# Routing attention with an MLP behind it: another start for the first batch

## Chip, cores, metric

One core of a Trainium2 chip runs the whole program. The metric is the device time in microseconds (us). The five engines are TensorE (PE), VectorE (DVE), ScalarE (ACT), GpSimd (POOL) and SyncE (SP), which here issues the DMA transfers.

## What is computed

The reference, cut to what matters. There are 4 batches, 8 heads, 768 tokens, 64 channels per head and 16 clusters; the MLP has 512 x 2048 weights.

```python
q_assign = argmax(einsum('bhsd,hcd->bhsc', q_n, c_n))   # normalised q and centroids
k_assign = argmax(einsum('bhsd,hcd->bhsc', k_n, c_n))
mask = q_assign[:, :, :, None] == k_assign[:, :, None, :]
scores = where(mask, q @ k.T / 8, -1e9)
attn = exp(scores - max(scores)); attn = attn / (sum(attn) + 1e-9)
x = (attn @ v) laid out as (tokens, heads * channels)
h = x @ w_in
g = where(h > 0, h, exp(min(h, 0)) - 1)
out = g @ w_out
```

A token of q sees a token of k only where both have the same nearest centroid. The weights come in as doubles and are turned into single floats on the chip.

## The kernel before

**Blocks.** Attention works on 48 blocks: a batch, a third of its 768 queries (256) and a pair of heads (`pr`, four of them). The 768 keys of a block are three units of two key tiles of 128. `scores(n)` fills one PSUM tile of two banks per unit: for each key tile and each head of the pair (`e`) the plain product of k and q (L406), then the product of the one-hot clusters of k with the masked one-hot clusters of q (L415), which adds zero where the clusters agree and minus 2^80 where not. ScalarE takes the exponential of the whole unit (L423). `values(n)` sums values and row sums over the six key tiles on TensorE (L452, L441), copies them out on ScalarE (L466, L468), takes the reciprocal on VectorE (L469) and scales on GpSimd (L470). The MLP runs seven blocks behind.

**The first batch.** `turn(i, j)` brings channels on partitions for pair `i` of q (`j` = 0) or k (`j` = 1). For later batches VectorE does that (L316); for the first batch TensorE does. The two heads of q lie apart in the loaded tile, so each tile of 128 tokens and each head is a product of its own with the identity as the moving operand (L326), 12 products of 64x128 in a pair. They appear as 24 records in the profile, since a product of 32-bit floats makes two. k lies with both heads side by side, so 6 true transposes of 128x128 make up a pair (L322). One ScalarE copy of 128x768 then brings the pair into SBUF (L329).

**Clusters.** `similar(b, j, half)` multiplies the turned pairs with the centroids for half of the tokens (384 columns, L337), four pairs into one bank, and VectorE transposes blocks of 32x32 out of PSUM (L344). `assign(b, j, half)` takes the largest of 16 (L354), compares (L356, which also counts), transposes the one-hot result (L366) into `hot[:, 0]` and copies it to the other half of the partitions (`hot[:, 1]`, two copies, L369), since a head may need its partner's side. `masks(n)` makes the masked one-hot of q for a block on ScalarE (`qm`, L380, one for each head).

**Order.** Each engine works its instructions off in the order in which the program writes them, and semaphores tie the engines together. The program is written by hand: for q, then for k, four `turn`, then for each half `similar` and `assign`; `masks(0)` after q. Then the loop over blocks begins, with `masks(1)` ahead of `scores(0)`. PSUM tiles of two banks come from a pool of three (`banks()`), handed out in turn: a product into a new one waits until whoever read its predecessor is done.

**Weights.** `weigh(n)` runs n steps of the conversion of weights, each of five VectorE operations (L246, L249, L252, L260, L268) and one ScalarE operation (L271) on 128x512. Up to block 9, one step is written after each unit of `scores`. Loads of q, k, v and weights are issued by SyncE in that order from 0.75 us on; a q pair is 384 KB, a k pair two transfers of 192 KB.

Of the kernel before, what the change touches and what calls it, by code (L numbers as in the profile page):

```python
# [9 lines left out]
F32 = mybir.dt.float32  # L10
BF16 = mybir.dt.bfloat16
U32 = mybir.dt.uint32
I32 = mybir.dt.int32
Act = mybir.ActivationFunctionType
Alu = mybir.AluOpType
# [3 lines left out]
P = 128  # L19
# [41 lines left out]
def main_path(ctx, tc, c, q, k, v, centroids, moe_w_in, moe_w_out, out):  # L61
    nc = tc.nc
    B, H, S, D = q.shape
    NC = centroids.shape[1]
    DM, DF = moe_w_in.shape
    NT = S // P
    HT = NT // 2
    HS = S // 2
    NQ = 3
    QS = S // NQ  # L70
    QT = NT // NQ
    NPR = H // 2
    KC = DM // P
    FC = DF // P
    SCALE = 1.0 / 8.0
# [18 lines left out]
    def banks():  # L94
        return short.tile([P, 2, 512], F32, name="banks", tag="banks")
# [47 lines left out]
    cen, ident = c["cen"], c["ident"]  # L143
# [49 lines left out]
    nc.tensor.transpose(cps[:, :P], cen2.rearrange("p e d -> p (e d)"), ident)  # L193
    cT = const.tile([P, P], F32, name="cT")
    nc.vector.tensor_copy(cT, cps[:, :P])
    count = const.tile([P, 4 * B], F32, name="count")
    r_sum = const.tile([P, NQ * len(pairs)], F32, name="r_sum")
    d_sum = const.tile([P, NQ * len(pairs)], F32, name="d_sum")

# [81 lines left out]
    def weigh(n):  # L281
        for _ in range(n):
            next(rest, None)
# [28 lines left out]
    def turn(i, j):  # L312
        T[i, j] = turned.tile([P, S], F32, name=f"{name_of[j]}T", tag="turned")
        src = raw[name_of[j], i]
        if i >= NPR:
            nc.vector.transpose(T[i, j], src)  # L316
            return
        ps = banks()
        for t in range(NT):
            to = ps[:, t // HT, ts(t % HT, P)]  # L320
            if j == 1:
                nc.tensor.transpose(to, src[:, t].rearrange("p h d -> p (h d)"), ident)  # L322
                continue

            for e in range(2):
                nc.tensor.matmul(  # L326
                    to[64 * e : 64 * e + 64], lhsT=src[:, e, t], rhs=ident, start=True, stop=True
                )
        nc.scalar.copy(T[i, j].rearrange("p (h s) -> p h s", h=2), ps[:, :, :HS])  # L329

    def similar(b, j, half):
        if half == 0:
            sim[b, j] = route.tile([P, S], F32, name="sim", tag="sim", bufs=1)
        ps = banks()[:, 0]
        cols = slice(half * HS, (half + 1) * HS)
        for pr in range(NPR):
            nc.tensor.matmul(  # L337
                ps[32 * pr : 32 * pr + 32, :HS],
                lhsT=cT[:, 32 * pr : 32 * pr + 32],
                rhs=T[b * NPR + pr, j][:, cols],  # L340
                start=True,
                stop=True,
            )
        nc.vector.transpose(sim[b, j][:, cols], ps[:, :HS])  # L344

    def assign(b, j, half):
        if half == 0:
            hot[b, j] = route.tile([P, 2, S], BF16, name="hot", tag=f"hot{j}", bufs=1 + j)
        cols = slice(half * HS, (half + 1) * HS)
        n = HS // NC  # L350
        s = sim[b, j][:, cols].rearrange("p (n c) -> p n c", c=NC)
        top = route.tile([P, n], F32, name="top", tag="top", bufs=1)
        oh = route.tile([P, HS], BF16, name="oh", tag="oh", bufs=1)
        nc.vector.tensor_reduce(top, s, axis=Axis.X, op=Alu.max)  # L354
        at = 4 * b + 2 * j + half
        nc.vector.scalar_tensor_tensor(  # L356
            oh.rearrange("p (n c) -> p n c", c=NC),
            s,
            1.0,
            top.unsqueeze(2).to_broadcast([P, n, NC]),  # L360
            op0=Alu.mult,
            op1=Alu.is_equal,
            accum_out=count[:, at : at + 1],
        )
        h = hot[b, j]
        nc.vector.transpose(h[:, 0, cols], oh)  # L366
        for e in range(2):
            at = 64 * e
            nc.vector.tensor_copy(h[64 - at : 128 - at, 1, cols], h[at : at + 64, 0, cols])  # L369

    def side(pr, e):
        return int(pr // 2 != e)

    def masks(n):
        b, third, pr = blocks[n]
        qm[n] = route.tile([P, QS], BF16, name="qm", tag="qm", bufs=2)
        for e in range(2):
            rows = slice(64 * e, 64 * e + 64)
            m = big[rows, pr % 2 : pr % 2 + 1]
            nc.scalar.activation(  # L380
                qm[n][rows],
                hot[b, 0][rows, side(pr, e), ts(third, QS)],
                Act.Identity,
                scale=m,
                bias=minus[rows, pr % 2 : pr % 2 + 1],
            )
# [9 lines left out]
    def scores(n):  # L396
        b, third, pr = blocks[n]
        i = b * NPR + pr
        cols = ts(third, QS)
        for u in range(NT // 2):  # L400
            s = banks()
            for m in range(2):
                kt = 2 * u + m
                for e in range(2):
                    rows = slice(64 * e, 64 * e + 64)
                    nc.tensor.matmul(  # L406
                        s[:, e, ts(m, QS)],
                        lhsT=T[i, 1][rows, ts(kt, P)],
                        rhs=T[i, 0][rows, cols],
                        start=True,  # L410
                        stop=False,
                    )
                for e in range(2):
                    rows = slice(64 * e, 64 * e + 64)
                    nc.tensor.matmul(  # L415
                        s[:, e, ts(m, QS)],
                        lhsT=hot[b, 1][rows, side(pr, e), ts(kt, P)],
                        rhs=qm[n][rows],
                        start=False,
                        stop=True,  # L420
                    )
            p = pu[n, u] = probs.tile([P, 2, 2 * QS], F32, name="p", tag="p")
            nc.scalar.activation(p, s, Act.Exp, scale=SCALE)  # L423
            if n < LAG + 3:
                weigh(1)

# [187 lines left out]

    seen = {0}
    raw["v", 0] = raw.pop(("v", 0))
    for j in range(2):
        for pr in range(NPR):
            turn(pr, j)
        for half in range(2):  # L620
            similar(0, j, half)
            assign(0, j, half)
        if j == 0:
            masks(0)

    for n in range(len(blocks) + LAG):
        b, at = n // NB, n % NB
        ahead = b + 1 < B
        if n <= len(blocks) and n > 0:
            values(n - 1)  # L630
        if ahead:
            for pr in {5: [0], 6: [1], 9: [2], 10: [3]}.get(at, []):
                load("q", (b + 1) * NPR + pr)
                load("k", (b + 1) * NPR + pr)
        if n + 1 < len(blocks):
            load_v(n + 1)
        if n + 1 < len(blocks) and at + 1 < NB:
            masks(n + 1)
        if n < len(blocks):
            scores(n)  # L640
        if 0 < n <= len(blocks):
            check(n - 1)
        if n < len(blocks):
            if n >= LAG + 3:
                sums(n)
            if ahead and at in turns:
                for j in range(2):
                    turn((b + 1) * NPR + turns[at], j)
        beside = []
        if ahead and at + 1 == NB:  # L650
            beside.append(None)
            for j in range(2):
                beside.append(lambda b=b, j=j: [similar(b + 1, j, half) for half in range(2)])
                beside.append(lambda b=b, j=j: [assign(b + 1, j, half) for half in range(2)])
            beside.append(lambda n=n: masks(n + 1))
        main = groups[n - LAG] if n >= LAG else []
        if n == LAG + 2:
            weigh(100)
            for half in range(2):
                sum_weights(half)  # L660
        done = 0
        for m, step in enumerate(main):
            step()
            upto = len(beside) * (m + 1) // len(main)
            for other in beside[done:upto]:
                if other:
                    other()
            done = upto
            if n < LAG + 2:
                weigh(1)  # L670
        for other in beside[done:]:
            if other:
                other()

    ok = c["ok"]
    peak = const.tile([P, 2], F32, name="peak")
    same = const.tile([P, 4 * B], F32, name="same")
    nc.vector.tensor_reduce(peak[:, 0:1], r_sum, axis=Axis.X, op=Alu.add)
    nc.vector.tensor_reduce(peak[:, 1:2], d_sum, axis=Axis.X, op=Alu.add)
    nc.vector.tensor_scalar(ok[:, 0:1], peak[:, 0:1], R_MAX, None, op0=Alu.is_lt)  # L680
    nc.vector.tensor_scalar(ok[:, 1:2], peak[:, 1:2], D_MAX, None, op0=Alu.is_lt)
    nc.vector.tensor_scalar(same, count, float(HS // NC), None, op0=Alu.is_equal)
    nc.vector.tensor_reduce(ok[:, 2:3], same, axis=Axis.X, op=Alu.min)
    nc.vector.tensor_reduce(ok[:, 3:4], ok[:, 0:3], axis=Axis.X, op=Alu.min)
    ps = banks()[:, 0]
# [256 lines left out]
```

## Time and profile before

The median of three runs is 1041.45 us (1040.57 to 1042.23). The profiled span is 1040.0 us.

| First batch, from the timelines of the engines | us |
|---|---|
| first transfer issued | 0.75 |
| TensorE starts on q (L326) | 5.69 |
| last copy of turned q begins (ACT L329) | 12.71 |
| VectorE begins on q's clusters (L344) | 14.43 |
| TensorE starts on k (L322) | 14.97 |
| VectorE begins on k's clusters (L344) | 21.92 |
| exponentials of block 0 begin (L423) | 25.52, 27.84, 29.52 |
| first value product (L452) | 28.82 |
| first reciprocal (DVE L469) | 34.77 |

How to read it: the rows are start times on different engines, and each depends on the one above. A timeline row gives start, duration, engine, line, operation, output and inputs. The groups by line give the number of instructions, the total time and the mean of one. The chain of waits follows the last instruction back to what released it, step by step; of an engine's work it shows only what lay on that path.

### The profile page before, as it was taken

Reading aid. Unit: us, or ns where it says so; the run is one execution under the profiler, and the core shown is the slowest. Engines: PE = TensorE matmul, PEld = TensorE weight load, DVE = VectorE, ACT = ScalarE, POOL = GpSimd, SP = SyncE. Lnnn points to the kernel's source line nnn. Section 1 sums busy time; section 2 is a strip of 40 time slices with the busy share of each in tenths; the row PEclk is TensorE's granted clock in tenths of the full one; section 3 lists DMA queues with packets and bytes.
Section 4 is the critical chain, followed back from the end, with each engine's and each line's share of the span. In section 5 each row is a group of like instructions: output and inputs, shape, how many; then the busy total and the mean of one; then the engine's idle time right before and its main releaser. Section 6 shows DMA issues by size and latency. Waiting matters only on the chain.

```text
span 1040.0 us, 14929 instructions
## 1 busy us (share of the span) xinstructions
PE 1004.5 (97%) x6403; PEld 781.9 (75%) x6403; DVE 515.9 (50%) x670; ACT 343.5 (33%) x595; POOL 115.8 (11%) x129
## 2 busy tenths in 40 slices
PE   6999988999999999999999999999999999999996
PEld 4656766777877777778778778777877877888885
DVE  4899895564343444574344246375324424423031
ACT  4676432233323332333332242234224223321010
POOL 0010121110110110111011011011011011011010
PEclk9999998999999999999999999999999999999999
DMA  9748230101122122100122103200011011000000
GB/s 288 283 120 238 63 65 21 36 16 32 36 46 48 50 44 48 51 16 16 51 46 46 38 29 56 51 24 30 16 36 31 17 36 31 16 21 1 21 1 23
DMA packets 103961, 55.60 MB, mean 53 GB/s; under 512 B 83408, under 2 KB 96720, under 8 KB 103888
## 3 DMA queue, kind: packets, MB, share of 16 engines
q1 hardware_dynamic: 103888, 54.57, 19.4%
q8 instruction: 52, 0.85, 0.3%
q14 instruction: 21, 0.17, 0.0%
HBM read 48.27 MB, written 6.29 MB: 52 GB/s over the span
## 4 chain that ended last, share of the span: by engine, by line
PE 85%; DVE 10%; ACT 3%; issue 1%; DMA 0%; POOL 0%; SPq 0%; ACTq 0%; DVEq 0%
PE banks L491 31%; PE f_bank L521 16%; PE o_bank L521 12%; PE o_bank L452 11%; PE banks L406 9%; PE banks L441 2%; PE banks L415 2%; DVE ex L246 1%; DVE r L469 1%; DVE w_in L249 1%; ACT qm L380 1%; DVE w_in L252 1%; ACT p L423 1%; PE banks L337 1%; DVE ex L268 1%; DVE w_out L249 1%
## 5 line engine op out<-in xcount | busy, mean ns | idle before, releaser
L491 PE MATMUL banks<-xT,w_in 128*128 128x256 f32 x1536 | 338.4, 381 | 0.6 <-ACT p L423 0.3
L491 PEld LDWEIGHTS banks<-xT,w_in 128*128 128x128 f32 x1536 | 289.8, 190 | 48.2 <-issue 4.2
L406 PE MATMUL banks<-qT,kT 64*128 64x256 f32 x1152 | 166.1, 388 | 4.7 <-ACT p L423 4.7
L452 PE MATMUL o_bank<-p,v_raw 128*64 128x256 f32 x1152 | 143.8, 384 | 4.8 <-ACT p L423 4.7
L423 ACT ACTIVATE p<-banks 128x1024 f32<-128x1024 f32 x144 | 140.6, 1021 | 12.6 <-PE banks L415 11.0
L469 DVE RECIPROCAL r<-r 128x256 f32<-128x256 f32 x48 | 84.0, 1750 | 119.4 <-ACT r L468 119.3
L501 ACT ACTIVATE gT<-banks 128x1024 f32<-128x1024 f32 x48 | 49.2, 1025 | 283.9 <-PE banks L491 283.9
L508 DVE SCALAR_TENSOR_TENSOR gT<-gT,banks 128x1024 f32<-128x1024 f32 x48 | 58.4, 1216 | 155.3 <-POOL gT L502 155.2
L406 PEld LDWEIGHTS banks<-qT,kT 64*128 64x128 f32 x1152 | 87.6, 187 | 53.5 <-PE o_bank L452 10.4
L452 PEld LDWEIGHTS o_bank<-p,v_raw 128*64 128x64 f32 x1152 | 78.1, 137 | 57.7 <-issue 16.4
L521 PE MATMUL o_bank<-w_out,gT 128*128 128x256 f32 x384 | 91.0, 391 | 7.2 <-POOL w_out L302 7.2
L466 ACT COPY xT<-o_bank 128x256 f32<-128x256 f32 x48 | 17.7, 370 | 218.8 <-PE o_bank L452 218.8
L521 PEld LDWEIGHTS o_bank<-w_out,gT 128*128 128x128 f32 x384 | 73.5, 194 | 21.4 <-POOL w_out L302 8.3
L502 POOL TENSOR_SCALAR gT<-gT 128x1024 f32<-128x1024 f32 x48 | 51.2, 1067 | 342.0 <-ACT gT L501 342.0
L521 PE MATMUL f_bank<-w_out,gT 128*128 128x256 f32 x384 | 86.8, 379 | 0.0
L470 POOL TENSOR_TENSOR xT<-xT,r 128x256 f32<-128x256 f32 x48 | 39.7, 827 | 414.2 <-DVE r L469 414.2
L415 PE MATMUL banks<-qm,hot 64*128 64x256 bf16 x576 | 80.0, 269 | 2.0 <-DVE hot L366 2.0
L521 PEld LDWEIGHTS f_bank<-w_out,gT 128*128 128x128 f32 x384 | 73.0, 190 | 9.9
L429 DVE TENSOR_TENSOR psum<-p 128x1024 f32<-128x1024 f32 x38 | 47.0, 1236 | 42.5 <-ACT p L423 42.5
L380 ACT ACTIVATE qm<-hot,minus,big 64x256 bf16<-64x256 bf16 x96 | 56.7, 591 | 4.1 <-DVE hot L366 3.3
L430 DVE TENSOR_TENSOR psum<-psum,p 128x1024 f32<-128x1024 f32 x38 | 46.8, 1231 | 6.1 <-ACT p L423 2.6
L521 PE MATMUL f_bank<-w_sum,g_sum 128*128 128x256 f32 x192 | 44.6, 386 | 1.2 <-DVE part L568 1.2
(107 smaller groups left out, 773.6 us busy)
## 6 DMA issues: line engine op xcount, KB each, us to landing
v_raw<-in_v_dram SPq DMA_DIRECT2D x48, 384.0 KB, 3.2
w_sum<-in_moe_w_out_dram SPq DMA_DIRECT2D x12, 512.0 KB, 4.3
out_dram<-o_sb SPq DMA_DIRECT2D x24, 256.0 KB, 2.0
q_raw<-in_q_dram SPq DMA_DIRECT2D x48, 96.0 KB, 3.5
k_raw<-in_k_dram SPq DMA_DIRECT2D x48, 96.0 KB, 3.4
w_sum<-in_moe_w_in_dram SPq DMA_DIRECT2D x8, 512.0 KB, 7.4
w_out<-in_moe_w_in_dram SPq DMA_DIRECT2D x8, 512.0 KB, 10.7
w_out<-in_moe_w_out_dram SPq DMA_DIRECT2D x4, 512.0 KB, 3.9
```

Of the source, the lines that this page charges most:

```text
L380: nc.scalar.activation(qm[n][rows], hot[b, 0][rows, side(pr, e), ts(third, QS)], Act.Identity, scale=m, bias=minus[rows, pr % 2 : pr % 2 + 1],
L406: nc.tensor.matmul(s[:, e, ts(m, QS)], lhsT=T[i, 1][rows, ts(kt, P)], rhs=T[i, 0][rows, cols], start=True, stop=False,)
L415: nc.tensor.matmul(s[:, e, ts(m, QS)], lhsT=hot[b, 1][rows, side(pr, e), ts(kt, P)], rhs=qm[n][rows], start=False, stop=True,)
L423: nc.scalar.activation(p, s, Act.Exp, scale=SCALE)
L429: nc.vector.tensor_tensor(to, pu[n, 0], pu[n, 1], op=Alu.add)
L452: nc.tensor.matmul(o_bank[64 * e : 64 * e + 64, :QS], lhsT=raw["v", n][:, e, kt], rhs=p[:, e, ts(m, QS)], start=(kt == 0), stop=(kt == NT ...
L469: nc.vector.reciprocal(r, r)
L491: nc.tensor.matmul(hf[:, f], lhsT=w_in[:, ch, ts(4 * n + f, P)], rhs=xT[b, third][:, ch], start=(ch == 0 and f % 2 == 0), stop=(ch == KC - 1),
L501: nc.scalar.activation(t, hf, Act.Exp)
L502: nc.gpsimd.tensor_scalar(t, t, 1.0, 0.0, op0=Alu.min, op1=Alu.max)
L508: nc.vector.scalar_tensor_tensor(t, t, -1.0, hf, op0=Alu.add, op1=Alu.max)
L521: nc.tensor.matmul(to[:, :QS], lhsT=left[:, f], rhs=right[:, f], start=(f == 0), stop=(f == FC // 2 - 1),)
```

## The change

It concerns the first batch alone, in four parts.

1. *q is turned by transposes of two tokens.* In q's loaded tile the 64 channels of a token are followed by those of the next one, so 128 columns are two tokens of one head. Six transposes of 128x128 replace the twelve products of a pair. Even tokens come out on the lower 64 partitions, odd ones on the upper, for one head in each bank, so four copies of 64x384 put them in place: for each head one by ScalarE and one by VectorE.
2. *The order.* Both stream transposes of q's cluster products come ahead of both assignments, and the four turns of k stand between them in the program. `similar` returns its VectorE part, to be written where wanted.
3. *Clusters of k by thirds.* The clusters of k are found for 256 tokens at a time, each third being what one unit of scores needs. The stream transposes are of 256 and 512 columns. The copies to the other side are ScalarE's for these thirds.
4. *Scores ahead.* The plain products of units 0 and 1 of block 0 are written ahead of the clusters, those of unit 2 after the second third; the mask products follow. The three conversion steps of block 0 come after its three units.

It is meant to take work off TensorE at the start, and to let block 0 begin before all clusters of k are known. At the end, the count of one-hot entries is compared in two pieces, since thirds and halves have different counts.

```diff
+        for e in range(2):
+            for t in range(HT):
+                nc.tensor.transpose(
+                    ps[:, e, ts(t, P)],
+                    src[:, e, 2 * t : 2 * t + 2].rearrange("p t d -> p (t d)"),
+                    ident,
+                )
+        for e in range(2):
+            for m in range(2):
+                to = T[i, j][64 * e : 64 * e + 64].rearrange("p (t m n) -> p t m n", m=2, n=P)
+                of = ps[64 * m : 64 * m + 64, e, :HS].rearrange("p (t n) -> p t n", n=P)
+                if m == 0:
+                    nc.scalar.copy(to[:, :, m], of)
+                else:
+                    nc.vector.tensor_copy(to[:, :, m], of)
...
-        nc.vector.transpose(sim[b, j][:, cols], ps[:, :HS])
+        return lambda: nc.vector.transpose(sim[b, j][:, cols], ps[:, :size])
...
         for e in range(2):
             at = 64 * e
-            nc.vector.tensor_copy(h[64 - at : 128 - at, 1, cols], h[at : at + 64, 0, cols])
+            if size == QS:
+                nc.scalar.copy(h[64 - at : 128 - at, 1, cols], h[at : at + 64, 0, cols])
+            else:
+                nc.vector.tensor_copy(h[64 - at : 128 - at, 1, cols], h[at : at + 64, 0, cols])
...
+        if n == 0:
+            turn_first = similar(0, 1, 0, QS)
+            turn_rest = similar(0, 1, QS, 2 * QS)
+            units = [banks() for _ in range(2)]
+            for u in range(2):
+                for m in range(2):
+                    plain(units[u], 2 * u + m)
+            turn_first()
+            for u in range(NT // 2):
+                assign(0, 1, u * QS, QS)
+                if u == 0:
+                    turn_rest()
+                    masks(0)
+                if u == 1:
+                    units.append(banks())
+                    for m in range(2):
+                        plain(units[2], 4 + m)
+                for m in range(2):
+                    mask(units[u], 2 * u + m)
+                exponentials(units[u], u)
+            weigh(3)
+            return
...
-    for j in range(2):
-        for pr in range(NPR):
-            turn(pr, j)
-        for half in range(2):
-            similar(0, j, half)
-            assign(0, j, half)
-        if j == 0:
-            masks(0)
+    for pr in range(NPR):
+        turn(pr, 0)
+    for half in range(2):
+        similar(0, 0, half * HS, HS)()
+    for pr in range(NPR):
+        turn(pr, 1)
+    for half in range(2):
+        assign(0, 0, half * HS, HS)
...
-    nc.vector.tensor_scalar(same, count, float(HS // NC), None, op0=Alu.is_equal)
+    for size, at in counted.items():
+        cols = slice(at[0], at[-1] + 1)
+        nc.vector.tensor_scalar(
+            same[:, cols], count[:, cols], float(size // NC), None, op0=Alu.is_equal
+        )
```

## The prediction

> **What bounds the kernel now.** I read the shares first: TensorE (PE) is busy 97% of the span and owns 85% of the chain that ended last.
>
> ```profile
> PE 1004.5 (97%) x6403; PEld 781.9 (75%) x6403; DVE 515.9 (50%) x670; ACT 343.5 (33%) x595; POOL 115.8 (11%) x129
> PE 85%; DVE 10%; ACT 3%; issue 1%; DMA 0%; POOL 0%; SPq 0%; ACTq 0%; DVEq 0%
> ```
>
> The change leaves everything after block 0 alone, so the average says little. I turned to the chain of waits in order of time, first 80 us:
>
> ```profile
> 5.76 6.93 PE banks L326 x96
> 12.71 0.81 ACT qT L329
> 13.56 0.85 PE banks L337 x5
> 14.43 0.59 DVE sim L344
> ...
> 16.85 0.60 ACT qm L380
> 17.48 0.59 ACT qm L380
> 18.09 0.81 ACT kT L329
> 18.95 0.88 PE banks L322 x6
> 19.82 2.08 PE banks L337 x11
> 21.92 0.59 DVE sim L344
> ...
> 34.27 0.48 ACT r L468 x2
> 34.77 1.75 DVE r L469
> 36.53 0.55 DVE ex L246
> ```
>
> Columns: start, length, engine and line. The start-up is one relay: PE turns q (to 12.7), ACT copies the last qT (to 13.51), PE and DVE find q's clusters, ACT makes masks and only then copies kT, DVE finds k's clusters from 21.92, PE and ACT score block 0. From the reciprocal at 34.77 on, the chain stays on DVE (weight conversion, L246 to L268) until about 89 us and then passes to PE. DVE is first in, first out, so a shift d of the first reciprocal shifts the rest by d. The PE timeline puts the first value product (L452) at 28.82, 5.95 ahead of that reciprocal. **So the question is only when block 0's value products can start.**
>
> Three rows of ScalarE's timeline matter too:
>
> ```profile
> 18.09 2.91 ACT L329 COPY kT<-banks 128x768 f32<-128x768 f32 x4
> 21.03 1.21 ACT L380 ACTIVATE qm<-hot,minus,big 64x256 bf16<-64x256 bf16 x2
> 22.25 1.28 ACT L423 ACT_TABLE_LOAD   x1
> ```
>
> The table load ends at 23.53, while the first exponential starts at 25.52, held by a mask product: today the load is hidden.
>
> [...]PE starts at 5.31, the first 48 records of L326 need 4.18 us (5.69 to 9.87) and the next 48 only 2.72; the switch lies near 8.8. [...]the cluster products (L337) last 486 ns at 12.6 and at 19.8, with only transposes between them. [...]
>
> **The change, part by part.**
>
> *Turning q, PE.* 96 records become 24 transposes. Like transposes (L322, k) run 6 in about 0.70 at full clock, 0.117 each; I take about 0.21 at half clock (double; if weight loads set the pace at 0.12, the first pair is 0.55 earlier). Pair 0 is turned at 5.69 + 6 x 0.21 + 0.2 = 7.2. 24 of them take 5.0 against 6.9 now, but the copies decide.
>
> *Turning q, copies.* One ACT copy of 128x768 (0.80) per pair becomes four of 64x384: ACT, DVE, ACT, DVE. As built, each waits for the one before: every VectorE copy waits for ACT's, and ACT's second waits for VectorE's first. An ACT copy costs 0.48 (between the rows of 0.37 for 256 and 0.80 for 768 columns), a VectorE copy 0.56 (0.29 for 128 columns out of PSUM in L195, plus 256 at 1.04 ns, the slope between VectorE's rows of 512 and 1024 columns, 0.69 and 1.22), a handover 0.03. The last copy of a pair runs beside the first of the next, so a pair takes 0.48 + 0.56 + 0.56 + 0.1 = 1.70; the last needs 2.18. The last qT is ready at 7.2 + 3 x 1.70 + 2.18 = **14.5, where it is 13.51 now**. With the early pair 0 and copies 10% shorter it is 13.4. PE's saving is lost: the copies are the path.
>
> *Clusters of q.* As today, DVE starts 0.92 later (15.4). Both stream transposes now come first (second ends at 14.5 + 1.57 + 0.6 = 16.6), then both assignments, 2.26 each as from 15.05 to 17.31 now: DVE is free at 21.2. Same work, shifted by 1.0.
>
> *Turning k.* PSUM buffers come free early and the copies no longer queue behind masks. k0 starts at 16.0; the four copies (0.8 each, in series) end at 20.1, against 21.0 now, and the first third's cluster product at 20.6. The loads do not hold this: the last k half is issued at 11.1 and lands 5.2 later, at 16.3, and k3 is turned at about 17.7. But DVE is busy until 21.2, so this costs and gains nothing by itself.
>
> *First third of k.* Transpose to clusters takes 2.40 for 384 columns (21.92 to 24.32); four operations lose 128 columns each, 0.133 by the same slope, so 1.87: **ready at 23.1, 24.32 now**. That is the gain of the change, 1.2 us. The other thirds (0.75 + 2 x 1.3) lie beside ACT's work below.
>
> *Early scores.* Units 0 and 1 before the clusters: 16 records at 0.107, 1.7 us. PE had idle time there (1.20 and 0.78 ahead of the mask products), which ACT now fills; worth nothing on the path.
>
> *ACT behind the first third.* Its order as built: two copies of the clusters (moved from DVE), two masks of block 0, table load, exponential 0, two copies, exponential 1, two copies, exponential 2. A 64x256 copy is 0.40, two 0.71 (0.413 for L476; the mask's 0.591 has two pointer operands more). Each third's copy is queued behind the exponential before it, and the mask product of that unit waits for it. Sum from 23.1: 0.03 + 0.71 + 1.21 (masks) + 1.28 (load, no longer hidden) + 1.02 (exponential 0) + 0.40 (first copy) + 0.6 (mask products) + 1.02 + 0.40 + 0.4 (mask products issued) = 7.1. The value products start at **30.2, against 28.82: +1.4**. Exponential 2 ends near 31.4, in time for the fifth key tile 3.5 later.
>
> *Weights.* Three conversion steps of block 0 come after exponential 2: ACT's first at 32.1, DVE done at 34.8, before the reciprocal at 36.1. Nothing.
>
> *End.* `same` is made by two small operations instead of one, on the path to `go`: +0.1 (small operations there follow each other 0.1 apart).
>
> Sum: 1041.45 + 1.4 + 0.1 = **1042.9**.
>
> **The rivals.** *(a) The clock stays at half speed.* PE loses its 96 matmuls, and the copies spread what remains from 10 to 14.5. [...]q's second cluster product ends about 1.1 later, k's transposes take 1.3 per pair instead of 0.7, and the last kT copy and the product behind it slip to about 24: the first third comes 2.8 later, and early scores at 0.21 per record bring up to 1 more. [...]against it: no relapse between 15.0 and 19.8 today. 1042.9 + 2.8 = **1045.7**: slower. *(b) The relay is tighter than I think:* copies overlap in spite of the waits, q is ready by 11.5, k's loads (16.3) then limit, and the first third comes near 20. 28.82 becomes 26.9, **1039.5**. For it: PE is done with q early; against it: the waits as built. [...]
>
> **How the numbers follow.** Forecast 0.50, (a) 0.30, (b) 0.10, (c) 0.10. The bound of 0.2% is 2.1 us: 1039.4 and 1043.5. The forecast, with copies short or transposes quick, reaches down to 1041.7, and with longer handovers up to 1044: of its 0.50, 0.37 falls within, 0.12 above, 0.01 below. (a) gives 0.28 slower, 0.02 same; (b) 0.06 faster and 0.04 same; (c) 0.08 slower, 0.02 same. Sum: faster 0.07, same 0.45, slower 0.48. The range 1040.4 to 1046.2 leaves out most of (b) and the top of (a).
>
> **What would show it.** Alternating ACT and DVE copies of qT with PE waiting, the last ending near 14.5; L337's first third taken up by DVE only when q's assignments end near 21; the table load directly before exponential 0, which waits for no matmul; each later mask product released by an ACT copy; value products near 30, first reciprocal near 36. I am wrong if the qT copies overlap (then faster), or if matmuls of 384 columns last well over 486 ns after 14 us (then (a)).

## The result, and the profile after

The changed kernel takes 1045.97 us (median of four runs, 1045.37 to 1046.75), the kernel before 1041.84 us beside it (1040.57 to 1042.83). The ratio is 1.0041, with a 95% interval of 1.0023 to 1.0058: the change costs 4.1 us. The forecast was 1042.9 us; the range reached to 1046.2.

The top of the page says as little as it did before. TensorE has 72 records fewer (6331 against 6403), and the time is longer.

```profile
PE 1004.2 (96%) x6331; PEld 779.9 (75%) x6331; DVE 519.2 (50%) x679; ACT 346.2 (33%) x605; POOL 116.1 (11%) x129
```

The chain of waits of the changed kernel, in order of time (start, length, engine, line):

```profile
5.71 1.29 PE banks L331 x6
7.03 0.48 ACT qT L341
...
13.69 0.57 DVE qT L343
...
14.31 1.49 PE banks L352 x10
...
20.97 0.37 DVE sim L359
...
22.77 0.40 ACT hot L387
...
29.57 0.60 PE banks L436 x2
30.17 1.05 PE o_bank L506 x4
31.22 0.85 PE banks L495 x4
...
38.66 1.75 DVE r L523
```

Read it against the chain before. q's relay now runs through alternating copies on ScalarE and VectorE and ends at 14.26 (13.51 before). VectorE turns to the first third of k at 20.97, when q's assignments are done. The third is ready at 22.77, 1.55 earlier than all of the first half was. Then ScalarE holds the chain until 30.1, but for some short mask products of TensorE, and the value products begin 1.3 later than before. But the reciprocal comes at 38.66, against 34.77: 3.9 later. The value products themselves, which the change doesn't touch, became longer: groups of four records now take 0.85 us.

ScalarE's timeline behind the first third shows what fills the 7 us. In brackets: idle time before the row, and what ended it.

```profile
22.77 0.82 ACT L387 COPY hot<-hot 64x256 bf16<-64x256 bf16 x2 [2.15 <-DVE hot L383]
23.60 1.22 ACT L400 ACTIVATE qm<-hot,minus,big 64x256 bf16<-64x256 bf16 x2
24.83 1.28 ACT L447 ACT_TABLE_LOAD   x1
26.13 1.02 ACT L447 ACTIVATE p<-banks 128x1024 f32<-128x1024 f32 x1
```

The masks and the load of the table stand behind the copies, although ScalarE was idle for 2.15 us just ahead of them. Exponential 0 follows the load at once: nothing but ScalarE's own queue holds it.

Why did the value products become longer? The busy times by stretches of 5 us, first of the kernel before, then of the changed one. The columns of interest are the first, PE busy (records), and the one behind POOL, the granted clock of TensorE.

```profile
25.00:30.00 5.00, 4.21 (x42) 2.60 (x40) 4.37 (x12) 3.16 (x4) 0.00 (x0) 1.00 1.02 418
30.00:35.00 5.00, 5.00 (x48) 3.24 (x46) 2.54 (x6) 2.24 (x6) 0.00 (x0) 1.00 1.03 403
```

```profile
25.00:30.00 5.00, 1.95 (x19) 0.98 (x16) 2.23 (x8) 4.77 (x7) 0.00 (x0) 0.86 1.02 408
30.00:35.00 5.00, 5.00 (x25) 2.81 (x26) 2.66 (x5) 2.36 (x3) 0.00 (x0) 0.50 1.01 396
```

While ScalarE works off its queue, TensorE is busy for 1.95 us of 5 instead of 4.21. The clock then falls to half, at 28.59, and stays there until 35.42, through the first half of the value products: 25 records in 5 us instead of 48.

Not all of the 3.9 us reaches the end. At the reciprocal of a block near 116 us (116.43 before, 120.28 after) the shift is 3.85; when TensorE goes on with value products after the sums of weights (168.46 and 171.35) it is 2.89. In that stretch both kernels wait twice for GpSimd (4.53 and 2.69 us before, 4.55 and 2.17 after) and lose the clock. The kernel before has it at half speed for 10.24 us in a row there (155.60 to 165.84), the changed one twice for 3.41 (from 158.30 and from 165.13) with as long at full speed between: eight products take 3.78 us before and 3.00 after. (The expectations below count such stretches in windows of 3.41 us, the length of the shortest.) How much comes back there differs between the profiles: 0.75 to 1.25 us in ten of the eleven kernels with the changed order, this one among them, and 0.1 in x_hl. At `go`, near the end, the shift is 2.65; `same` takes 0.57 instead of 0.50.

The spans tell 1042.9 us against 1039.9 (medians; the second is that of the kernel before beside the first experiments), so 3.0 of the 4.1 us. The rest lies outside: device time less span is 3.27 us in the changed kernel and 2.06 in the one before. That was the second surprise.

### The profile page after: what moved, and what is told of

Same layout as the page of the kernel before. It is cut to its first block, busy times and chain, and to the rows that moved or that the text cites. A ratio compares the mean times of both kernels' runs of the same rounds, so it can differ in the third digit from the quotient of the medians.

```text
span 1043.1 us, 14804 instructions
## 1 busy us (share of the span) xinstructions
PE 1004.2 (96%) x6331; PEld 779.9 (75%) x6331; DVE 519.2 (50%) x679; ACT 346.2 (33%) x605; POOL 116.1 (11%) x129
## 4 chain that ended last, share of the span: by engine, by line
PE 84%; DVE 11%; ACT 3%; issue 1%; POOL 0%; DMA 0%; ACTq 0%; DVEq 0%
PE banks L545 31%; PE f_bank L575 16%; PE o_bank L575 12%; PE o_bank L506 11%; PE banks L424 9%; PE banks L495 3%; PE banks L436 2%; DVE ex L248 1%; DVE r L523 1%; ACT p L447 1%; DVE w_in L251 1%; ACT qm L400 1%; DVE w_in L254 1%; PE banks L352 1%; DVE ex L270 1%; DVE w_out L251 1%
## 6 DMA issues: line engine op xcount, KB each, us to landing
w_out<-in_moe_w_in_dram SPq DMA_DIRECT2D x8, 512.0 KB, 10.2
```

## The experiments

The theory after the result had three terms: (1) ScalarE's queue behind the first third delays the value products; (2) the starved TensorE loses its clock, and the value products run at half speed; (3) something outside the span costs about 1.2 us. The rivals: the clock is lost because TensorE has fewer products in turning q, or q's copies are what matters. Times below are medians against the kernel before on the same chip (1041.7 to 1041.9 us, span 1039.7 to 1039.9, 2.06 to 2.09 outside).

**Fillers for TensorE, first try (x_fill).** Five products ahead of each unit's mask products.

```diff
+                for _ in range(5):
+                    nc.tensor.matmul(
+                        f_bank[:, :QS], lhsT=ident, rhs=T[0, 0][:, :QS], start=True, stop=True
+                    )
                 for m in range(2):
                     mask(units[u], 2 * u + m)
```

> The changed kernel with five products of 128x128 by 128x256 into the unused f_bank ahead of the mask products of each of block 0's three units; their results are read by nobody. They fit into TensorE's idle stretches there (1.25, 1.6 and 1.5 us; five take about 1.1) and change no other engine's work. Theory (starved clock: ScalarE's queue starves TensorE between 23 and 30 us, and the halved clock from 28.5 to 35.4 costs 2.4 us): no relapse, value products still start near 30.1, first reciprocal near 36.2 instead of 38.66, and 2.4 us less than the changed kernel, about 1043.5. Rival (the lost q products: what TensorE no longer does before 15 us leaves the clock on edge, or the relapse is chance): the clock halves at about the same time, the reciprocal stays at 38.7 and the time at 1046.

Measured: 1045.01 us, ratio 1.0026 (1.0016 to 1.0037), span 1042.9. Five fillers took 2.43 us instead of 1.1: they are ten records of 0.24 each. That pushed the value products to 31.88. The clock stayed full, though (1.00 from 20 to 40 us), and the value products took 5.2 us. Inconclusive in time, so fewer fillers were tried next.

**Two fillers (x_fill2).** The same with `range(2)`.

> As the first filling experiment, but two products into f_bank ahead of each unit's mask products instead of five: five took 2.4 us and held the mask products up. Two take about 0.97 and fit into stretches of 1.25, 1.5 and 1.5 us. Theory: value products start within 0.3 of 30.1, the clock stays full through them, they take 5.2 us instead of 7.6, first reciprocal near 36.2 instead of 38.66; span near 1041, unless the clock loses a window more where the weights are summed. Rival: the clock halves near 28.5 all the same and nothing is gained.

Measured: 1042.48 us, ratio 1.0007 (0.9999 to 1.0015), span 1040.3. TensorE's timeline at the value products, first of the changed kernel, then with fillers:

```profile
30.10 1.12 PE L506 MATMUL o_bank<-p,v_raw 128*64 128x256 f32 x4
31.01 1.07 PE L495 MATMUL banks<-p,ones 128*64 128x256 f32 x4
```

```profile
29.82 0.65 PE L510 MATMUL o_bank<-p,v_raw 128*64 128x256 f32 x4
30.31 0.60 PE L499 MATMUL banks<-p,ones 128*64 128x256 f32 x4
```

The products start within 0.3 of each other and follow one another at 0.43 instead of 0.85. TensorE was busy for 4.48 us of the 5 from 25 to 30, the clock stayed at 1.00, and the reciprocal came at 35.78 instead of 38.66. So it was TensorE's idleness (busy for 1.95 us of those 5 without the fillers) that took the clock here: added work of no use made the kernel faster. This shows term (2). In the medians of the span it is worth 2.6 us against the changed kernel, and 1.7 against x_pad below, which is the changed kernel with a tail.

**Copies of the clusters back on VectorE (x_dve).**

```diff
-            if size == QS:
-                nc.scalar.copy(h[64 - at : 128 - at, 1, cols], h[at : at + 64, 0, cols])
-            else:
-                nc.vector.tensor_copy(h[64 - at : 128 - at, 1, cols], h[at : at + 64, 0, cols])
+            nc.vector.tensor_copy(h[64 - at : 128 - at, 1, cols], h[at : at + 64, 0, cols])
```

> The changed kernel with the copies of k's clusters to the other side given back to VectorE; all else stays. Theory: ScalarE's masks and the table load then run while VectorE finds the first third, so exponential 0 starts at about 23.8 instead of 26.13, exponential 1 at 26.3 and the value products at 27.7 instead of 30.10; TensorE is busy enough for the clock to stay full; reciprocal near 33.7, about 5 us below the changed kernel and 1 us below the one before: 1041. Rival (the q part is what costs): masks come earlier, but the clock still halves near 28.5, reciprocal near 36, and 2.4 us or less are gained.

Measured: 1042.51 us, ratio 1.0005 (0.9997 to 1.0014), span 1039.0. Masks and load now ran in ScalarE's idle time, and exponential 0 began at 23.58 instead of 26.13. The value products began at 28.11. The clock fell all the same (0.73, 0.50, 0.50 and 0.56 in the four us from 27 to 31), so the reciprocal came at 35.41, not at 33.7, and the time was 1042.5, not 1041: the span is 0.9 us under that of the kernel before, but 3.76 us lie outside it. Term (1) holds; the assumption that an earlier start also keeps the clock did not.

**Masks and load ahead of the copies (x_load).** The same wait attacked without touching who copies.

```diff
             turn_first()
+            masks(0)
+            early = const.tile([P, 1], F32, name="early")
+            nc.scalar.activation(early, ones[:, :1], Act.Exp)
             for u in range(NT // 2):
...
-                    masks(0)
```

> The changed kernel with block 0's masks and the load of the exponential table ahead of the copies of k's clusters on ScalarE (an exponential of one column there brings the load forward; its result is read by nobody). The copies stay ScalarE's. Theory (ScalarE's queue behind the first third is the path): exponential 0 starts at about 24.4 instead of 26.13, the value products at 28.3 instead of 30.10; the wait of each later unit for its copy stays, so TensorE is as sparse as before and the clock is halved for one or two windows. First reciprocal between 35.5 and 37, some 2 us below the changed kernel. Rival (the queue was slack, the thirds of k on VectorE set the units): value products within 0.5 of 30.1.

Measured: 1042.60 us, ratio 1.0009 (1.0001 to 1.0018), span 1040.1. ScalarE's timeline:

```profile
21.83 1.28 ACT L460 ACT_TABLE_LOAD   x1
23.13 0.20 ACT L460 ACTIVATE early<-ones 128x1 f32<-128x1 f32 x1
23.36 0.83 ACT L387 COPY hot<-hot 64x256 bf16<-64x256 bf16 x2
24.24 1.02 ACT L447 ACTIVATE p<-banks 128x1024 f32<-128x1024 f32 x1
```

The load is over before the third's copies begin, and exponential 0 comes at 24.24. Value products began at 28.00, the reciprocal at 33.95, ahead of the kernel before. The clock stayed full (1.00 from 20 to 40), where one or two windows at half speed had been expected; but this profile is one of the shortest executions of this kernel (span 1038.4, median 1040.1), so the others may not have kept it. The time is 1.4 us better than was expected. So term (1) was not the thirds and not the copies as such, but 2.5 us of masks and load queued behind a late operand.

**q turned as before, the rest of the change kept (x_qold)**: the new branch of `turn` taken out.

> The changed kernel with q turned as before: 96 product records and one ScalarE copy per pair; all else stays. Theory: last qT at 13.5 instead of 14.25, everything up to the value products 0.75 earlier (29.35), the clock halves all the same since ScalarE's queue is the same, reciprocal near 37.9: 0.75 us less than the changed kernel, 1045.2. Rival (lost q products): the clock stays full, the reciprocal comes near 35.3 and the time near 1042.8.

Measured: 1043.01 us, ratio 1.0013 (1.0005 to 1.0021), span 1041.2. The last qT was ready at 14.56 in its profile, not at 13.5: the first 48 records that turn q took 5.17 us there (5.58 to 10.75), against 4.18 in the kernel before. Value products began at 30.44, and the clock fell all the same (0.58 from 28 to 29, 0.50 to 34, 0.51 to 35); the reciprocal came at 38.62. The 72 records taken from q's turn are not what lost the clock. The time outside the span was 2.02 here, as before. The time came out 2.2 us under the forecast; 1.25 us of the difference to the changed kernel lie outside the span, and why the median span is 1.7 us shorter, this profile (span 1042.5) doesn't show.

**The new turn of q alone, in the kernel before (x_qnew)**: only the new branch of `turn` put in.

> The kernel before with part 1 alone: q turned by 24 transposes and copied by ScalarE and VectorE in turn. Theory: last qT near 14.25 instead of 13.51, so everything up to the first reciprocal about 0.7 later, 35.5 instead of 34.77, and the clock stays full, since block 0 is fed as before; span 1040.6. The program is as short as the changed one, so the time outside the span, 2.05 in the kernel before and 3.3 to 3.8 in the changed one, is expected at the upper value: 1044.2 in all. Rival (fewer products of q starve the clock by themselves): clock halved between 20 and 36 us, reciprocal at 37 or later.

Measured: 1043.17 us, ratio 1.0012 (1.0005 to 1.0019). Last qT at 14.25, value products at 29.57, reciprocal at 35.53, clock full (1.00 from 15 to 40). The median span, 1039.3, is no longer than before, where 1040.6 was expected: the 0.76 us at the reciprocal, still 0.72 near 142 us in the profile (span 1040.8), don't reach it, and the reason isn't shown. The device time is 1.5 us longer because 3.72 us lie outside. This part alone brings term (3).

**q's copies split by head (x_heads).** ScalarE copies both parities of one head, VectorE both of the other.

```diff
-                if m == 0:
+                if e == 0:
                     nc.scalar.copy(to[:, :, m], of)
```

> The changed kernel with the four copies of turned q shared out by head (both of head 0 to ScalarE, both of head 1 to VectorE) instead of by even and odd tokens; all else stays. As built, VectorE's two still wait for ScalarE's two, but ScalarE goes on to the next pair without waiting. Theory: a pair takes 1.15 instead of 1.70, last qT near 12.6 instead of 14.25, first third of k near 21.2 instead of 22.7, value products near 28.5, clock halved all the same, reciprocal near 37.0: 1.6 us less than the changed kernel, 1044.4. Rival (the loads of k or VectorE's other work hold the clusters anyway): first third within 0.3 of 22.7, no gain.

Measured: 1044.44 us, ratio 1.0020 (1.0014 to 1.0027), span 1040.7. VectorE's timeline, where the changed kernel stands idle for 0.54 between the two copies of each pair:

```profile
9.24 1.13 DVE L343 COPY qT<-banks 64x384 f32<-64x384 f32 x2 [0.15 <-ACT qT L341]
10.61 2.28 DVE L343 COPY qT<-banks 64x384 f32<-64x384 f32 x4 [0.25 <-ACT qT L341]
13.88 1.23 DVE L359 STREAM_TRANSPOSE sim<-banks 128x384 f32<-128x384 f32 x2 [0.99 <-PE banks L352]
```

VectorE's two copies still wait for ScalarE's two of the same pair, but they now run beside those of the next pair. The relay ends 1.3 us earlier (13.88 against 15.18), and value products begin at 29.02. The clock still fell (0.68 from 26 to 27, 0.50 to 33, 0.91 to 34): reciprocal 37.01. The forecast of the time was met in part by chance: the first value product came 0.5 us later than was said, and 0.4 us more than in the changed kernel lie outside the span, while the median span fell by 2.2. Term (1) moves with the relay, term (2) stays.

**Fifteen products of one column at the end (x_pad).** The first runs fell into two kinds: the kernel before, x_fill and x_qold, with 6361 records or more on TensorE, had 2.0 to 2.1 us outside the span; the changed kernel, x_dve and x_heads, with 6331, had 3.3 to 3.8. So the changed kernel was given 30 records more, where they cost next to nothing.

```diff
+    for _ in range(15):
+        nc.tensor.matmul(ps[:1, 1:2], lhsT=ones[:, :1], rhs=ones[:, :1], start=True, stop=True)
```

> The changed kernel with fifteen products of one column ahead of the last product of the program, into a column that nobody reads; TensorE is idle there for 1.9 us. Device time minus span was 2.05 us wherever TensorE had 6361 or 6403 products in the profile, and 3.3 to 3.8 with 6331; this one has 6361. Theory (the rest of the loss outside the span hangs on the length of TensorE's program): time minus span is 2.05, the span stays within 0.5 of 1042.9, and the time is 1045.0, 1 us less than the changed kernel. Rival (that time belongs to the new order of work, or to the chip): it stays above 3.2.

Measured: 1044.17 us, ratio 1.0025 (1.0014 to 1.0036), span 1042.0, outside 2.18. Term (3) went away. In this profile the clock was at half for 3.42 us rather than 6.83 (29.51 to 32.93; reciprocal at 37.43), although nothing ahead of that point differs from the changed kernel. The busy times in stretches of 3.41 us, laid on the points where the clock changed, first of the changed kernel, then with the pad:

```profile
25.18:28.59 3.41, 1.34 (x14) 0.67 (x11) 2.08 (x7) 3.29 (x5) 0.00 (x0) 1.00 1.01 404
28.59:32.01 3.42, 2.44 (x13) 1.28 (x15) 0.00 (x0) 3.07 (x6) 0.00 (x0) 0.50 1.04 415
```

```profile
26.10:29.51 3.41, 0.41 (x5) 0.11 (x4) 1.19 (x4) 3.26 (x6) 0.00 (x0) 1.00 1.03 407
29.51:32.93 3.42, 3.38 (x17) 1.83 (x19) 0.93 (x2) 2.76 (x4) 0.00 (x0) 0.50 1.03 410
```

In both a stretch with little work (busy for 1.34 and 0.41 us) is followed by one at half speed. In the changed kernel that one begins 1.5 us ahead of the value products, TensorE is busy for only 2.44 us of it, and a second one follows, to 35.42. With the pad the stretches lie 0.9 us later, the one at half speed is busy for 3.38, and the clock is full behind it (the mean from 30 to 35 us is 0.71, against 0.50). So the same order of work spent 6.83 us at half speed in one profile and 3.42 in the other; what sets the points where it changes isn't shown (more on this in the last section).

**The two edits together (x_hl), and with the pad (x_best).** Split by head, masks and load early; then the same with the fifteen products.

> The changed kernel with two edits together: the four PSUM copies of each turned q pair split between ScalarE and VectorE by head instead of by token parity (tried before with 21.46 us for the first third's end and 1044.4), and the first unit's masks and the load of the exponential's table put ahead of the copies of the thirds (tried before with value products from 28.0 and 1042.6). If block 0 is a relay whose gains add, the first third is ready at about 21.4, the value products start at 26.9 (28.0 less the 1.1 that the head split gave) and the reciprocal is at 32.9. TensorE waits less, so the clock should stay full to there. Span 1039.1, a microsecond under x_load's 1040.1; and since the program for TensorE keeps its 6331 records, the time outside the span should stay at 2.5 to 3.8 us: 1042.3 in all. If the two edits hit the same wait, value products start at 27.8 and it stays at 1042.6 to 1043.

> The same two edits, and fifteen products of one column behind the last transposes of the program, as in the run with the pad, so that TensorE's program has some 6361 records. If the time outside the span hangs on the length of that program, it is 2.0 to 2.2 us here against 2.5 to 3.8 in the kernel without the pad on the same chip, with the same span: 1041.2 in all, under the kernel before (1041.8). If the pad's effect in the earlier run was chance, the two agree, at 1042.3.

Measured: x_hl 1041.93 us, ratio 1.0001 (0.9993 to 1.0009), span 1038.3, outside 3.61. x_best 1040.61 us, ratio **0.9988 (0.9981 to 0.9995)**, span 1038.5, outside 2.06. Value products began at 26.92 and 26.65, reciprocals at 32.9 and 32.6: up to there the gains add up. Behind the reciprocal TensorE meets another limit: the load of v for block 1, for which the kernel before doesn't wait at all and x_load 0.48 us. In x_best:

```profile
37.93 0.65 PE L508 MATMUL o_bank<-p,v_raw 128*64 128x256 f32 x4 [2.42 <-DMA v_raw<-in_v_dram]
```

The wait is 1.9 us in x_hl. The clock falls to half behind it in x_best (39.17 to 42.58), and the second reciprocal comes at 45.62 there and 43.65 in x_hl, against 44.73 in the kernel before: the 2.2 us that x_best had gained at the first are gone, and of the 1.9 of x_hl 1.1 are left. (The profile of x_best is a long execution, span 1039.5, median 1038.5.) An earlier load of v was not tried. The first lines of the two pages, x_hl ahead of x_best:

```profile
PE 1002.7 (97%) x6331; PEld 780.9 (75%) x6331; DVE 519.1 (50%) x679; ACT 346.6 (33%) x606; POOL 116.1 (11%) x129
```

```profile
PE 1003.7 (97%) x6361; PEld 781.3 (75%) x6361; DVE 519.1 (50%) x679; ACT 346.8 (33%) x606; POOL 116.2 (11%) x129
```

Apart from the 30 records they are the same kernel, with the same span to 0.2 us, and the pad alone is worth 1.3 us. x_best is 1.2 us faster than the kernel before and the fastest kernel up to here.

**Fillers at the sums of weights, with the two edits (x_best_sum) and in the kernel before (x_sum).** Eleven products where TensorE waits 4.5 us for GpSimd.

```diff
+            for _ in range(11 if b == third == 0 else 0):
+                nc.tensor.matmul(
+                    o_bank[:, :QS], lhsT=ident, rhs=w_in[:, 0, :QS], start=True, stop=True
+                )
             product(o_bank, c_, f_)
```

> The same two edits, no pad at the end, but eleven filler products (128x128 by 128x256, written over by the product that follows) where TensorE waits 4.5 us for the first of GpSimd's two sums of weights, which bring TensorE's records to 6353. If the half-speed windows seen there in both kernels come from that wait, they vanish: the eight products after the second wait take 3.0 us instead of 3.8 and the sixteen after them 4.1 instead of 4.3, 1.0 us in all, and the time outside the span is 2.0 to 2.2 us as well: 1040.2. If the clock there hangs on the second wait of 2.2 to 2.7 us, or the fillers come late and push the products back, it is 1041.2 or more.

> The kernel before with the eleven filler products alone, ahead of the product that waits 4.5 us for GpSimd's first sum of weights. If the wait is what halves the clock there, 1.0 us is gained (3.78 to 3.0 and 4.33 to 4.13 us for the products after the second wait): 1040.8, span 1038.9, time outside the span unchanged at 2.05. If the fillers run past the wait's end, or the clock falls all the same, 1041.8 to 1042.3.

Measured: x_best_sum 1040.17 us, ratio **0.9982 (0.9975 to 0.9988)**, span 1038.1, outside 2.01; x_sum 1041.96 us, ratio 1.0005 (0.9999 to 1.0011), span 1040.0. TensorE's timeline in the kernel before, and with the fillers in it (x_sum):

```profile
154.74 2.98 PE L521 MATMUL o_bank<-w_out,gT 128*128 128x256 f32 x8 [4.53 <-POOL w_out L302]
160.42 3.78 PE L521 MATMUL o_bank<-w_out,gT 128*128 128x256 f32 x8 [2.69 <-POOL w_out L302]
```

```profile
154.99 1.94 PE L521 MATMUL o_bank<-w_out,gT 128*128 128x256 f32 x8
160.61 3.78 PE L521 MATMUL o_bank<-w_out,gT 128*128 128x256 f32 x8 [3.68 <-POOL w_out L302]
```

The fillers cover the first wait, but the products behind them then finish sooner and wait longer for the second sum: 3.68 instead of 2.69. The clock falls there (0.50 from 160 to 165), and the products after it take 3.78 as ever. My expectation for x_sum was wrong: the second wait decides. In x_best_sum the clock was at half for 3.4 us there, against 6.8 in x_best and 10.2 in x_hl and the kernel before; but x_sum shows a higher granted clock too (0.995 to 0.997 in its executions, mostly 0.991 to 0.994 in the kernel before) and is no faster. The lead of x_best_sum, 0.4 us over x_best, is too small to be put down to that.

## Why the prediction came out as it did

**Right: the relay up to the value products.** Pair 0 was turned near 7.0 (forecast 7.2), the last qT ready at 14.26 (14.5), q's assignments done at 20.97 (21.2), the last kT copy at 19.54 (20.1), the first third at 22.77 (23.1), the value products at 30.10 (30.2). The working behind them held: copies one behind the other because of their waits, k's first third held up by VectorE, the load no longer hidden. x_load and x_dve then confirmed this step: take masks and load off the chain, and the value products begin 2 us earlier, of the 2.5 that the two were priced at. The conversions of weights cost nothing, and `same` cost 0.07 where 0.1 was given.

**Mis-sized: the length of the value products.** The step was "the value products start at 30.2, against 28.82: +1.4" with everything behind it only shifted, the reciprocal at 36.1. From the first value product to the reciprocal it took 8.6 us instead of 5.95, so the shift at the reciprocal was 3.9, not 1.4. The forecast saw TensorE's idle time ahead of the mask products and priced it at nothing; that idle time, grown, took the clock. The fillers of x_fill2 took this term away. About 1.0 came back where weights are summed, which the forecast hadn't seen either. And "a shift d of the first reciprocal shifts the rest by d" held only as far as that stretch, and for delays: a gain there can be lost at the load of v, as x_best shows.

**Mis-sized: the time outside the span.** The sum added the change of the span to the device time, as if the rest were constant. It grew by 1.2 us. x_pad, and x_best against x_hl, show that products added on TensorE take that away: kernels with 6343, 6353, 6361, 6403 and 6425 records had 2.0 to 2.2 us, the six with 6331 had medians of 2.5 to 3.8. The number of records is not all of it, though: of the 13 executions of x_load, one program, eight had 2.2 to 2.75 us outside and five 3.7 to 4.0. Nor did any run add as many instructions on another engine, so it may be the length of the whole program. What happens there isn't shown. A queue for instructions (q8 of the page) carries 52 packets in the kernel before and 51 in the changed one; whether the time hangs on that isn't shown.

Together: +1.3 (start of the value products) + 2.6 (their length) − 1.0 (sums of weights) + 0.1 or so at the end makes 3.0 of span, and 1.2 outside makes 4.2; measured 4.1. The terms inside the span are those of one profile of each kernel.

**Luck.** The forecast itself reached up to 1044; the measured 1045.97 lies inside the stated range because that was stretched upwards for rival (a), and most of the 0.48 given to "slower" was (a)'s too. That the range held is luck: the clock was lost, but not where and not for the reason that (a) gave.

**The rivals.** (a) gave 1045.7 and the measured time is 1045.97, but its mechanism is false. It had the clock stay at half speed from the start. In the changed kernel TensorE does little but transpose at the start, and the clock rises: 12 records of pairs 0 and 1 take 2.75 us from 5.51 on, 6 take 0.85 from 8.13 on. The cluster products at 14 us run at full speed (486 ns each, as in the kernel before). The clock was lost 14 us later, for want of work. (b) did not happen: as built, the copies waited for one another. x_heads shows that another split lets the copies of neighbouring pairs overlap, but it brings 1.1 us at the value products, not the 3.3 of (b). (c), at 0.10, had more time than the load itself pass ahead of exponential 0. It is refuted: exponential 0 starts 0.02 us after the load's 1.28, and from the end of the last mask (24.82) to the exponential (26.13) there are 1.31 us in all.

No single idle time of TensorE between 22 and 30 us is over 1.54 us in the changed kernel, and yet the clock fell.

## What to carry to other kernels

Giving work to another engine in a start-up relay cost twice here, 1.3 us by the wait for that engine and 2.6 because TensorE, kept waiting (busy for 1.95 us of 5), had half its clock for the work behind the wait: ask whether it stays busy enough. Then look for the next limit before counting on a gain; here it was the load of v. Where an operand arrives late, look at what stands behind it in that engine's queue: 2.5 us of masks and table load that needed nothing new stood behind ScalarE's copies, and put ahead of them, where ScalarE was idle for 2.15 us, they let the value products begin at 28.00 instead of 30.10 (x_load). And compare the device time with the span; where they move apart, as here by 1.2 us, the cause is not in the timeline.

## What the hardware showed that was not expected

- Between the first and the last product the clock fell to half for 6.83 us (28.59 to 35.42) and twice for 3.41 (from 158.30 and from 165.13) in the changed kernel and for 10.24 (155.60 to 165.84) in the kernel before, and for 3.42 (29.51 to 32.93) ahead of the first reciprocal in x_pad. Where such a stretch begins varies: x_pad has the work of the changed kernel up to there and lost the clock 0.9 us later.
- In these profiles the clock went with TensorE's busy time just before. In stretches of 3.41 us laid on the points where the clock changed, TensorE was busy for 1.34, 0.00 and 1.25 us (changed kernel, from 25.18, 154.89 and 161.71), 0.86 (kernel before, from 152.19) and 0.41 (x_pad, from 26.10), and half speed followed; it was busy for 1.44 (kernel before, from 148.78) and 1.80 (changed kernel, from 21.77), and full speed followed. At half speed it was busy for 3.09, 3.41 and 3.41 (changed kernel, from 158.30, 32.01 and 165.13), 3.41 (kernel before, from 162.43) and 3.38 (x_pad, from 29.51), and full speed followed; for 2.44 (changed kernel, from 28.59) and for 2.12 and 2.01 (kernel before, from 155.60 and 159.02), and half speed went on. What decides isn't shown. A fixed stretch hides this: from 25 to 30 us TensorE is busy for 2.93 us in x_load at a clock of 1.00, and for 3.70 in x_best_sum at 0.66.
- A filler product of 128x128 by 128x256 is two records, 0.22 to 0.24 us each. The rows for the sums of weights show the same pace (16 records in 3.6 us), and would have told it ahead of x_fill.
- Thirty records more on TensorE take 1.1 us (x_pad against the changed kernel) and 1.55 us (x_best against x_hl) off the time outside the span. In the second pair the span is the same to 0.2 us.
